# Attention's products in 64-row, 32-column tiles of TensorE, and six banks shared by scores and maxima

## The chip, the core and the metric

The kernel runs on one core of one Trainium2 chip. The metric is the device time of one execution in microseconds (us). The core has five engines with a queue each: TensorE (PE, whose weight loads are shown as PEld), VectorE (DVE), ScalarE (ACT), GpSimd (POOL) and SyncE (SP, which issues nearly all transfers). They meet through semaphores. Matmul results land in PSUM, 8 banks of 128 partitions x 512 fp32 numbers; ACT and DVE read them there.

## The reference, cut to what matters

A transformer block over 2048 rows of 512 numbers: attention with 32 heads of 16 numbers, then a gated MLP with a spatial mixing matrix. The change is in the attention.

```
H = 32; Dh = D // H
qkv = (LN(x) @ wqkv).reshape(B, S, 3, H, Dh)
scores = einsum("bhqd,bhkd->bhqk", q, k) * Dh ** -0.5
p = softmax(scores, axis=-1)
o = einsum("bhqk,bhkd->bhqd", p, v)
h = x + o.reshape(B, S, D) @ wo
```

## The kernel before

Each number of q and k is carried as fp16 parts, so a head has 48 rows of contraction instead of 16. Two more rows subtract the largest score of a query, scaled, so that Exp can't overflow. One operand tile holds two heads at partitions 0 to 49 (t = 0) and two at partitions 64 to 113 (t = 1).

The attention is a loop over 512 units (8 groups of four heads, 4 blocks of 512 queries, 16 blocks of 128 keys), two units at a time: a **pair**. One block of 512 queries is 8 pairs. In each pair the program issues, in an order written out by hand in the list `PAIR`:

- 8 score products (tokens `s0` to `s7`, line 805): 50 rows x 128 keys by 512 queries, each into a bank of its own of the pool `ps_s` (3 banks in turn). ACT turns each into Exp (line 814), which is stored in SBUF as `pt`.
- 8 products for the row maxima of a later block of queries (tokens `M0` to `M7`, line 223): into four banks `m0` to `m3` in turn (`bank`, `ps_m`, and one bank of `ps_m3`). DVE reduces 6 of them (line 228), ACT takes the absolute value of one (line 233), and DVE joins that with the eighth in a two-input reduction (line 237) that ends with a read of its accumulator.
- the weighted values (`weigh`, line 830, tokens `H`, `H`, `P`): for two blocks of keys, four fp32 matmuls of 128 keys x 32 columns, one for each head of the group, which add up in one bank `pv` over all 16 blocks of keys. Token `H` does 256 of the 512 queries, `P` all.

After the last block of keys DVE copies `pv` to SBUF (`take`, line 840, token `out`), and SP stores it. POOL meanwhile prepares weights for the MLP (`work`), off this chain.

Every PSUM result has a tile of its own with one bank. Semaphores come from the tile framework: it orders any two instructions that use one tile when one of them writes it, and lets instructions on different tiles run freely. All engines run their queues in the order of the program.

The products for maxima run ahead: 11 of 256 sets are made before the loop (`LEAD`), so 245 pairs have all 16 products, one pair has 8 scores alone, and the last 10 pairs run in another form (`scores2`, line 823): two scores into one tile of two banks, and one Exp over 1024 numbers, between matmuls for the next layer (`make_h`, line 747).

Of the kernel before, what the change touches and what calls it, by code (L numbers as in the profile page):

```python
# [39 lines left out]
PAIR = "s0 M0 join s2 M4 M1 s1 H s3 invert M2 s5 M3 H out M5 s4 M7 turn s6 s7 M6 P".split()  # L40
# [19 lines left out]
def block_kernel(ctx: ExitStack, tc: tile.TileContext, x, wqkv, wo, w_in, w_sp4, b_sp, w_out, out):  # L60
# [144 lines left out]
    def max_pair(m):  # L205

        g, i = divmod(m, 8)
        hg, qb = divmod(g, NQ)
        q, k, w = qst[g], kst[hg % 2], uvs[hg % 2]
        if i == 0:
            mx[g] = sm.tile([P, 16, 4], F32, name="mx")
            nc.gpsimd.memset(mx[g][:, :8, 3:], LOW)
        c, p = slice(i % 4 * P, i % 4 * P + P), i // 4
        at = lambda t, e: mx[g][:, t * 8 + i, e:e + 1]

        def scores(t, keys, b):  # L220
            r = slice(RG * t, RG * t + KS)
            acc = bank(b)
            nc.tensor.matmul(acc, q[r, p, c], keys[r, p], start=True, stop=True)  # L223
            return acc

        def one(t, e, b):
            acc = scores(t, k[:, :, 512 * e:512 * e + 512], b)
            nc.vector.reduce_max(at(t, e if t else e - 1), acc, axis=AX.X)  # L228

        def minus(b):  # L230
            acc = scores(0, w[:, :, 512:], b)
            ab[0] = sm.tile([P, 512], F32, name="ab")
            nc.scalar.activation(ab[0], acc, AF.Abs)  # L233

        def plus(b):
            acc = scores(0, w[:, :, :512], b)
            nc.vector.tensor_tensor_reduce(ab[0], acc, ab[0], 0.5, LOW, ALU.add, ALU.max, at(0, 0))  # L237
# [12 lines left out]
        ab = {}  # L250
        four = [lambda b, e=e: one(1, e, b) for e in range(4)]
        two = [lambda b, e=e: one(0, e, b) for e in (2, 3)]
        return [four[0], two[0], two[1], minus, four[1], four[2], plus, four[3], finish]

# [533 lines left out]
    with ExitStack() as at:  # L788
# [4 lines left out]
        pp = at.enter_context(tc.tile_pool(name="pp", bufs=6))  # L793
        ps_v = at.enter_context(tc.tile_pool(name="ps_v", bufs=1, space=PSUM))
        inner = at.enter_context(ExitStack())
        ps_m3 = inner.enter_context(tc.tile_pool(name="ps_m3", bufs=1, space=PSUM))
        ps_s = inner.enter_context(tc.tile_pool(name="ps_s", bufs=3, space=PSUM))
        more.clear()
        more[3] = lambda: ps_m3.tile([P, 512], F32, name="m3")
        pv = {}  # L800

        def product(s, hg, qb, kb, p, t):

            r = slice(RG * t, RG * t + KM)
            nc.tensor.matmul(s, kst[hg % 2][r, p, kb * P:(kb + 1) * P],  # L805
                             qst[hg * NQ + qb][r, p, :], start=True, stop=True)

        def score(hg, qb, kb, p, t):
# [3 lines left out]
            s = ps_s.tile([P, 512], F32, name="s")  # L812
# [3 lines left out]
        def scores2(hg, qb, kb, p):  # L816

            pts[p, kb] = pp.tile([P, 2, 512], F32, name="pt")
            turn[0] += 1
            s = later[turn[0] % 3 != 1].tile([P, 2, 512], F32, name="s2")  # L820
# [4 lines left out]
        def weigh(hg, qb, kb, a=0, b=512):  # L825
            if kb == 0:
                pv[0] = ps_v.tile([P, 512], F32, name="pv")
            for j in range(4):
                c = (4 * kb + j) * VW
                nc.tensor.matmul(pv[0][32 * j:32 * j + 32, a:b], vst[hg % 2][:, c:c + 32],  # L830
                                 pts[j % 2, kb][:, j // 2, a:b], start=kb == 0, stop=kb == NB - 1,
                                 skip_group_check=True)
            if b == 512:
                for p in range(2):
                    del pts[p, kb]

        def take(hg, qb, pool=sm):

            o = pool.tile([P, 512], F32, name="og", bufs=2)
            nc.vector.tensor_copy(o, pv[0])  # L840
# [204 lines left out]
        for n in range(0, len(units), 2):  # L1045
# [15 lines left out]
            steps = max_pair(m) if m < 8 * HG * NQ else []  # L1061
            m += 1
            if not steps and not later:
                maxima.close()
                later.append(attn.enter_context(
                    tc.tile_pool(name="ps_l", bufs=1, space=PSUM, side="right")))
                steps_h.append(make_h(h_rows[0], later[0].tile([P, 512], F32, name="h")))
            elif not steps and len(later) == 1:
                inner.close()
                later.append(at.enter_context(tc.tile_pool(name="ps_t", bufs=2, space=PSUM)))  # L1070
# [13 lines left out]
            if len(later) == 2:  # L1084
                if turned:
                    max_rows()
                more_h = n in (492, 494, 508, 510)
                scores2(hg, qb, kb, 0)
                scores2(hg, qb, kb, 1)
                some_h(1 + more_h)  # L1090
                weigh(*prev)
                if ends:
                    take(*prev[:2])
                scores2(hg, qb, kb1, 0)
                scores2(hg, qb, kb1, 1)
                some_h(1)
                weigh(hg, qb, kb)
            first = True
            for tok in PAIR if len(later) < 2 else ():
                i = int(tok[-1]) if tok[-1].isdigit() else 0  # L1100
                if tok[0] == "s":
                    score(hg, qb, (kb, kb1)[i // 4], i % 4 // 2, i % 2)
                elif tok[0] == "M" and steps:
                    steps[i](count[0] % 4)
                    count[0] += 1
                    if i == 6:
                        joins.append(steps[8])
                elif tok == "join":
                    join()
                elif tok == "H" and prev is None:  # L1110
                    if first:
                        pv[0] = ps_v.tile([P, 512], F32, name="pv")
                        for j in range(4):
                            nc.tensor.matmul(pv[0][32 * j:32 * j + 32, :], vst[0][:, :32],
                                             vst[0][:, :512], start=True, stop=True)
                    first = False
                elif tok == "H":
                    a = 0 if first else 256
                    weigh(*prev, a, a + 256)
                    first = False  # L1120
                elif tok == "P":
                    weigh(hg, qb, kb)
                elif tok == "out" and ends:
                    take(*prev[:2])
                elif tok == "invert" and kb == 6 and n > NB:
                    invert()
                elif tok == "turn" and turned:
                    max_rows()
            prev = (hg, qb, kb1)
# [8 lines left out]
            if n == 500:  # L1138
                steps_h.append(make_h(h_rows[1], later[0].tile([P, 512], F32, name="h")))
            if n == 502:  # L1140
                new_hn(h_rows[0])
        weigh(*prev)
# [461 lines left out]
```

## Time and profile before

| | |
|---|---|
| time, median of 3 runs | 1713.79 us (1713.14 to 1713.97) |
| span of the profiled execution | 1712.3 us, about 1.5 us less than the median time |
| before the attention's loop | 0 to 160 us |
| the 245 pairs with scores and maxima | 160 to 1249 us |
| 11 last pairs of the attention | 1249 to 1294 us |
| the MLP | from 1294 us on |

The page gives each engine's busy share, the span in 40 slices, the chain of work that ended last, and groups of instructions by line. A group's row has: line, engine, operation, output <- inputs, shapes and count, then busy us and mean ns of one, then the idle time of the engine just before them and who ended it. A row of the timeline has: start, length, engine, line, operation, and how many instructions were merged into it; merged ones overlap, so the length of a row divided by its count is less than one instruction takes. "PEclk" is the granted clock of TensorE as a share of full speed.

### The profile page before, as it was taken

How to read it: one execution, taken by the hardware profiler on the slowest of the kernel's cores; microseconds unless marked ns; L12 is line 12 of the kernel's file. 1: busy time of each engine (PE TensorE's matmuls, PEld its weight loads, DVE VectorE, ACT ScalarE, POOL GpSimd, SP SyncE). 2: the span in 40 equal slices, each digit the busy share in tenths (PEclk: the TensorE clock that was granted, in tenths of full speed). 3: DMA queues.
4: the chain of work that ended last, by engine and by line, in shares of the span. 5: the costliest groups of instructions: out<-in, count | busy, mean ns of one | idle time of the engine just before them, and what ended most of it. 6: DMA issues, size and time to landing. Idle time of an engine off the chain costs nothing.

```text
span 1712.3 us, 36689 instructions
## 1 busy us (share of the span) xinstructions
PE 1699.5 (99%) x13508; PEld 644.7 (38%) x13508; DVE 1452.5 (85%) x3051; ACT 1317.5 (77%) x2584; POOL 813.6 (48%) x1062
## 2 busy tenths in 40 slices
PE   9999999999999999999999999999999999999999
PEld 4533222222222222222222222222225666656665
DVE  7688999999999999999999999999936787543444
ACT  4334999999999999999999999999995545211111
POOL 1231867776673267687767776400002766300100
PEclk9999999999999999999999999999999999999999
DMA  5534332342221244344434444300114454664551
GB/s 185 167 94 144 103 89 68 101 94 82 81 68 25 56 118 117 104 144 125 130 113 124 132 140 130 80 13 19 37 39 124 140 173 140 233 234 156 198 217 44
DMA packets 189309, 196.03 MB, mean 114 GB/s; under 512 B 67496, under 2 KB 140008, under 8 KB 189128
## 3 DMA queue, kind: packets, MB, share of 16 engines
q1 hardware_dynamic: 186824, 188.04, 36.8%
q10 hardware_dynamic: 2304, 5.64, 0.8%
q8 instruction: 106, 1.74, 0.4%
q14 instruction: 75, 0.61, 0.1%
HBM read 122.10 MB, written 65.93 MB: 110 GB/s over the span
## 4 chain that ended last, share of the span: by engine, by line
PE 78%; DVE 12%; DMA 3%; POOL 2%; ACT 2%; SPq 2%; issue 1%; ACTq 0%; POOLq 0%; DVEq 0%
PE pv L830 26%; PE s L805 17%; PE m L223 9%; DVE mx L228 7%; PE acc L107 4%; PE g L108 4%; PE g L109 4%; PE g L107 4%; PE acc L109 4%; PE acc L108 4%; DMA rc<-r_scr 1%; DVE ab L237 1%; DVE og L840 1%; SPq L723 1%; DVE rs_t L124 1%
## 5 line engine op out<-in xcount | busy, mean ns | idle before, releaser
L814 ACT ACTIVATE pt<-s 128x512 f32<-128x512 f32 x1968 | 1006.2, 637 | 5.5 <-PE m L223 4.3
L228 DVE TENSOR_REDUCE mx<-m 128x1 f32<-128x512 f32 x1510 | 947.5, 682 | 11.7 <-PE m L223 2.9
L805 PE MATMUL s<-qst,kst 50*128 50x512 f16 x2048 | 604.2, 379 | 0.2
L830 PE MATMUL pv<-pt,vst 128*32 128x256 f32 (+1 forms) x6056 | 598.1, 466 | 4.1 <-DVE og L840 1.3
L223 PE MATMUL m<-kst,qst 48*128 48x512 f16 x1510 | 452.4, 381 | 0.0
L805 PEld LDWEIGHTS <-kst 50*128 50x128 f16 x2048 | 132.0, 94 | 352.1 <-issue 323.7
L830 PEld LDWEIGHTS pv<-pt,vst 128*32 128x32 f32 x6056 | 119.5, 108 | 290.7 <-issue 277.3
L223 PEld LDWEIGHTS <-qst 48*128 48x128 f16 x2048 | 159.2, 93 | 173.6 <-issue 124.2
L223 PE MATMUL m<-uvs,qst 48*128 48x512 f16 x504 | 190.5, 380 | 0.6 <-DVE mx L228 0.6
L245 POOL TENSOR_SCALAR nm<-nm 128x16 f32<-128x16 f32 x32 | 6.6, 206 | 358.8 <-DVE nm L242 358.8
L237 DVE CUSTOM_DVE_ANT_0 ab<-m,ab 128x512 f32<-128x512 f32 x252 | 170.5, 677 | 2.7 <-ACT ab L233 2.7
L233 ACT ACTIVATE ab<-m 128x512 f32<-128x512 f32 x252 | 157.3, 624 | 15.5 <-PE m L223 14.8
L1368 ACT ACTIVATE pr<-pr,up 128x304 f32<-128x304 f32 (+1 forms) x32 | 17.0, 574 | 109.2 <-DVE up L1322 109.2
L991 POOL TENSOR_TENSOR op<-raw,op 128x512 f16<-128x512 f32 x80 | 92.9, 1161 | 6.0
L914 POOL TENSOR_TENSOR raw<-raw 128x512 f32<-128x512 f32 (+1 forms) x84 | 83.3, 991 | 6.7
L919 POOL TENSOR_TENSOR acc_sp<-acc_sp,raw 128x512 f32<-128x512 f32 x63 | 80.4, 1277 | 4.5
L109 PE MATMUL acc<-wi,hT 128*128 128x344 f16 x256 | 79.1, 309 | 0.3 <-DVE hT L104 0.3
L107 PE MATMUL acc<-wi,hT 128*128 128x344 f16 x256 | 79.1, 309 | 0.0
L108 PE MATMUL acc<-wi,hT 128*128 128x344 f16 x256 | 79.1, 309 | 0.0
L1510 POOL TENSOR_TENSOR pr<-pr,z 128x344 f32<-128x344 f32 x8 | 7.3, 914 | 145.9 <-DMA whole<-squares 108.3
L911 POOL TENSOR_SCALAR raw<-raw 128x512 f32<-128x512 f32 (+1 forms) x88 | 52.3, 594 | 19.7 <-DMA raw<-in_wqkv 12.4
L1509 DVE TENSOR_TENSOR pr<-g,v 128x344 f32<-128x344 f32 x8 | 4.1, 517 | 66.6 <-PE g L109 63.5
(247 smaller groups left out, 2292.9 us busy)
## 6 DMA issues: line engine op xcount, KB each, us to landing
raw<-in_w_sp SPq DMA_DIRECT2D x128, 256.0 KB
s_scr<-op SPq DMA_DIRECT2D x64, 256.0 KB
op<-s_scr SPq DMA_DIRECT2D x32, 512.0 KB
a_scr<-op SPq DMA_DIRECT2D x48, 256.0 KB
op<-a_scr SPq DMA_DIRECT2D x24, 512.0 KB
o_scr<-og SPq DMA_DIRECT2D x64, 128.0 KB
qst<-q_scr SPq DMA_DIRECT2D x192, 32.0 KB
kst<-k_scr SPq DMA_DIRECT2D x48, 128.0 KB
```

The costliest lines, as they stand in the source:

```text
L107: nc.tensor.matmul(ps, lh, rh, start=first, stop=False, **kw)
L108: nc.tensor.matmul(ps, lh, rl, start=False, stop=False, **kw)
L109: nc.tensor.matmul(ps, ll, rh, start=False, stop=last, **kw)
L223: nc.tensor.matmul(acc, q[r, p, c], keys[r, p], start=True, stop=True)
L228: nc.vector.reduce_max(at(t, e if t else e - 1), acc, axis=AX.X)
L233: nc.scalar.activation(ab[0], acc, AF.Abs)
L237: nc.vector.tensor_tensor_reduce(ab[0], acc, ab[0], 0.5, LOW, ALU.add, ALU.max, at(0, 0))
L805: nc.tensor.matmul(s, kst[hg % 2][r, p, kb * P:(kb + 1) * P], qst[hg * NQ + qb][r, p, :], start=True, stop=True)
L814: nc.scalar.activation(pts[p, kb][:, t, :], s, AF.Exp, scale=scales_[hg // 2])
L830: nc.tensor.matmul(pv[0][32 * j:32 * j + 32, a:b], vst[hg % 2][:, c:c + 32], pts[j % 2, kb][:, j // 2, a:b], start=kb == 0, stop=kb == NB - 1,
L914: pool.tensor_mul(got[0] if n else acc, got[0], got[0])
L991: chores.append((lambda: pool.tensor_sub(t[0][:, 1], of(), t[0][:, 0]), TT))
```

## The change

Four things change in the attention's loop; the last one follows from the others.

1. **Quarters.** A score product or maxima product is issued as four matmuls of 32 columns of the stationary operand (`by_quarters`), each onto 32 partitions of the result. With the 64-row halves that the operands already use, every product then has the form 64 rows x 32 columns.
2. **Two sums.** `weigh` splits the 128 keys of a block into keys 0 to 63 and 64 to 127 and adds each half up in a bank of its own (`pv0`, `pv1`), in halves of 256 queries. At the end of a block ACT copies `pv1` to SBUF (`take_half`), and DVE adds it to `pv0` (`take`) in place of its copy.
3. **Six banks in turn.** One tile `slots` of six banks takes the place of the three `s` banks and the four `m` banks. Each product takes the bank that was given out longest ago. In the last pairs two neighbouring banks are taken at once, and one bank is held for `make_h`.
4. **The order.** `PAIR` is written anew, with a second list `FIRST_PAIR` for the first pair of a block of queries. In the lists `N` is a product of the t = 1 heads that DVE reduces, `n` one of t = 0, `A` the product for ACT's absolute value and `C` the one for the two-input reduction; `Q0`, `Q1` and `R0`, `R1` are the two sums for the block of keys before and for this one.

```diff
-PAIR = "s0 M0 join s2 M4 M1 s1 H s3 invert M2 s5 M3 H out M5 s4 M7 turn s6 s7 M6 P".split()
+PAIR = "s1 s0 N n s3 Q0 Q1 s2 N A Q1 s4 N Q0 s5 n R1 C s7 R0 R1 s6 N turn R0 rows".split()
+FIRST_PAIR = "s1 n N s0 s2 Q1 Q0 s3 n Q1 Q0 half N s4 out A s5 N s6 R1 C R1 R0 s7 N turn R0".split()
+SLOTS = 6
...
+    class Slots:
+        def __init__(self, pool, n):
+            self.acc = pool.tile([P, n, 512], F32, name="slots")
+            self.used, self.now = [0] * n, 0
...
+        def one(self):
+            i = min(range(len(self.used)), key=self.used.__getitem__)
+            self.mark(i)
+            return self.acc[:, i, :]
...
+    def by_quarters(acc, left, right):
+        for c in range(4):
+            c = slice(32 * c, 32 * c + 32)
+            nc.tensor.matmul(acc[c], left[:, c], right, start=True, stop=True)
...
         def scores(t, keys, b):
             r = slice(RG * t, RG * t + KS)
-            acc = bank(b)
-            nc.tensor.matmul(acc, q[r, p, c], keys[r, p], start=True, stop=True)
+            if slots:
+                acc = slots.one()
+                by_quarters(acc, q[r, p, c], keys[r, p])
...
-        ps_s = inner.enter_context(tc.tile_pool(name="ps_s", bufs=3, space=PSUM))
+        slots = Slots(at.enter_context(tc.tile_pool(name="ps_s", bufs=1, space=PSUM)), SLOTS)
...
-            s = ps_s.tile([P, 512], F32, name="s")
+            s = slots.one()
             product(s, hg, qb, kb, p, t)
             nc.scalar.activation(pts[p, kb][:, t, :], s, AF.Exp, scale=scales_[hg // 2])
...
-            s = later[turn[0] % 3 != 1].tile([P, 2, 512], F32, name="s2")
+            s = slots.two()
...
-        def weigh(hg, qb, kb, a=0, b=512):
+        def weigh(hg, qb, kb, t, cols=256):
...
+            r, c = slice(RG * t, RG * t + RG), slice(a, a + cols)
             for j in range(4):
...
+                nc.tensor.matmul(pv[t][32 * j:32 * j + 32, c], vst[hg % 2][r, v:v + 32],
+                                 pts[j % 2, kb][r, j // 2, c], start=kb == 0 and not a,
+                                 stop=kb == NB - 1 and a + cols == 512,
+                                 tile_position=(RG * t, 32 * j), skip_group_check=True)
...
+        def take_half(pool=sm):
+            halves.append(pool.tile([P, 512], F32, name="half", bufs=1))
+            nc.scalar.activation(halves[0], pv[1], AF.Copy)
...
-            nc.vector.tensor_copy(o, pv[0])
+            nc.vector.tensor_add(o, pv[0], halves.pop())
...
-                elif tok == "H" and prev is None:
-                    if first:
-                        pv[0] = ps_v.tile([P, 512], F32, name="pv")
-                        for j in range(4):
-                            nc.tensor.matmul(pv[0][32 * j:32 * j + 32, :], vst[0][:, :32],
-                                             vst[0][:, :512], start=True, stop=True)
```

What the change does to the instructions is shown by the built programs, engine by engine. Each row is one instruction with its line (in the changed file `by_quarters` is line 237, the Exp line 851, the reductions lines 266 and 275, the absolute value line 271, `weigh` line 870), output <- inputs and size, and behind it the engines whose semaphores it waits for.

First PE, in a pair from the middle of the attention. Before, the products of the first group of a pair stand as follows; `s` and `m_...` are tiles of one bank, `kst` and `qst` the operands:

```order
L805 LDWEIGHTS kst_158
L805 MATMUL s<-qst,kst_158 128x512 [waits Activation_49]
L223 LDWEIGHTS qst
L223 MATMUL m_11665<-kst_158,qst 128x512 [waits DVE_49]
L223 LDWEIGHTS qst
L223 MATMUL m_11668<-kst_158,qst 128x512 [waits DVE_49]
L805 LDWEIGHTS kst_158
L805 MATMUL s<-qst,kst_158 128x512 [waits Activation_49]
L830 MATMUL pv<-pt,vst_156 32x256 x4
```

A score waits for ACT, whose Exp frees the `s` banks, and a maxima product for DVE, which frees the `m` banks. With the change, the end of a first pair of a block (tokens `s6`, `R1`, `C`, `R1`, `R0`, `s7`, `N`) has these rows, of which the second to fourth quarter of each product are left out:

```order
L237 MATMUL slots<-qst,kst_158 32x512 [waits DVE_49]
...
L870 MATMUL pv_19306<-pt,vst_156 32x256 x3
L237 LDWEIGHTS qst
L237 MATMUL slots<-uvs_159,qst 32x512 [waits Activation_49]
...
L870 MATMUL pv_19306<-pt,vst_156 32x256 x4
L870 MATMUL pv_19320<-pt,vst_156 32x256 [waits PE_49]
...
L237 MATMUL slots<-qst,kst_158 32x512 [waits DVE_49]
...
L237 MATMUL slots<-kst_158,qst 32x512 [waits Activation_49]
```

The engine that a product waits for is now the reader of the product issued just before it: `s6` waits for DVE (which reduces the `N` before it), `C` (the row with `uvs`) for ACT (Exp of `s6`), `s7` for DVE (which reduces `C`), and `N` for ACT (Exp of `s7`). The readers of the banks' contents of six products earlier would be, for `C`, DVE, and for `s7`, ACT. The counts that these semaphores must reach say the same: in the pairs with all 16 products every product waits for the instruction that reads the product before it.

Then ACT at the same stage. Before, one pair and the next:

```order
L814 ACTIVATE pt<-s 128x512 [waits PE_49] x8
L233 ACTIVATE ab<-m_3962 128x512 [waits PE_49]
L814 ACTIVATE pt<-s 128x512 [waits PE_49] x8
L233 ACTIVATE ab<-m_4031 128x512 [waits PE_49]
L814 ACTIVATE pt<-s 128x512 [waits PE_49] x8
```

With the change, one pair:

```order
L851 ACTIVATE pt<-slots 128x512 [waits PE_49]
L271 ACTIVATE ab<-slots 128x512 [waits DVE_49,PE_49]
L851 ACTIVATE pt<-slots 128x512 [waits PE_49,Activation_49]
L851 ACTIVATE pt<-slots 128x512 [waits DVE_49,PE_49]
L851 ACTIVATE pt<-slots 128x512 [waits DVE_49,PE_49,Activation_49]
L851 ACTIVATE pt<-slots 128x512 [waits PE_49]
```

An Exp waited for its product alone; now those behind a product that DVE reads wait for DVE as well, though they read another bank. On DVE the reductions turn from the first form into the second in the same way:

```order
L228 TENSOR_REDUCE mx<-m_12819 128x1 [waits PE_49]
L228 TENSOR_REDUCE mx<-m_12832 128x1 [waits PE_49]
L228 TENSOR_REDUCE mx<-m_12847 128x1 [waits PE_49]
L228 TENSOR_REDUCE mx<-m_12853 128x1 [waits PE_49]
L237 ISA ab,mx<-m_12863,ab 128x512 [waits PE_49,Activation_49]
```

```order
L266 TENSOR_REDUCE mx<-slots 128x1 [waits PE_49,Activation_49] x2
L266 TENSOR_REDUCE mx<-slots 128x1 [waits PE_49]
L266 TENSOR_REDUCE mx<-slots 128x1 [waits PE_49,Activation_49] x3
L275 ISA ab,mx<-slots,ab 128x512 [waits DVE_49,PE_49]
L275 ISA mx 128x1
```

All banks of scores and maxima are now parts of one tile, and the waits stand between neighbours in the program, whichever banks they use.

More of the change, by code (lines that the diff above doesn't have):

```diff
@@ L250, in max_pair @@
         ab = {}
[L251 to L252 removed]
+        four = [lambda b=None, e=e: one(1, e, b) for e in range(4)]
+        two = [lambda b=None, e=e: one(0, e, b) for e in (2, 3)]
+        if slots:
+            return {"N": four, "n": two, "A": [minus], "C": [plus], "end": finish}
         return [four[0], two[0], two[1], minus, four[1], four[2], plus, four[3], finish]
@@ new lines, in block_kernel @@
+                weigh(hg, qb, kb, 1, 512)
+                weigh(hg, qb, kb, 0, 512)
+            for tok in (FIRST_PAIR if ends else PAIR) if len(later) < 2 else ():
+                t = int(tok[-1]) if tok[-1].isdigit() else 0
+                if tok[0] == "s" and len(tok) == 2:
+                    score(hg, qb, (kb, kb1)[t // 4], t % 4 // 2, t % 2)
+                elif tok in ("A", "C", "N", "n"):
+                    if steps:
+                        steps[tok].pop(0)()
+                elif tok[0] == "Q" and prev:
+                    weigh(*prev, t)
+                elif tok[0] == "R":
+                    weigh(hg, qb, kb, t)
+                elif tok == "half":
+                    take_half()
+                elif tok == "out":
+                    take(*prev[:2])
+                elif tok == "rows":
+                    join()
+                    if kb == 6 and n > NB:
+                        invert()
```

103 lines of the change are left out of this document (46 added, 57 removed).

## The prediction

> **What bounds the kernel now.** I read the engines' shares and the chain first, then the costliest groups.
>
> ```profile
> span 1712.3 us, 36689 instructions
> PE 1699.5 (99%) x13508; PEld 644.7 (38%) x13508; DVE 1452.5 (85%) x3051; ACT 1317.5 (77%) x2584; POOL 813.6 (48%) x1062
> PE 78%; DVE 12%; DMA 3%; POOL 2%; ACT 2%; SPq 2%; issue 1%; ACTq 0%; POOLq 0%; DVEq 0%
> L814 ACT ACTIVATE pt<-s 128x512 f32<-128x512 f32 x1968 | 1006.2, 637 | 5.5 <-PE m L223 4.3
> L228 DVE TENSOR_REDUCE mx<-m 128x1 f32<-128x512 f32 x1510 | 947.5, 682 | 11.7 <-PE m L223 2.9
> L823 ACT ACTIVATE pt<-s 128x1024 f32<-128x1024 f32 x40 | 37.6, 1021 | 0.9 <-ACT pt L814 0.3 <-PE s L805 0.2
> ```
>
> The chain runs through PE for 78% of the span. But the share of one stage counts here, so I asked for the busy time in a stretch of the attention.
>
> ```profile
> core 0: us, PE busy (x) PEld busy (x) DVE busy (x) ACT busy (x) POOL busy (x), PEclk, DMA share, GB/s
> 600.00:700.00 100.00, 99.66 (x904) 28.19 (x905) 99.25 (x194) 99.95 (x205) 72.66 (x104) 1.00 0.40 112
> ```
>
> PE, DVE and ACT are all above 99%: three engines in balance. Nothing that helps PE alone can be worth much, and anything that stops the three from working at the same time costs nearly all of what it stops. The timeline shows how they run side by side; first the stage's two ends and the fp32 product that opens a pair:
>
> ```profile
> 160.23 0.39 PE L805 MATMUL s<-qst,kst 50*128 50x512 f16 x1
> 604.31 1.06 PE L830 MATMUL pv<-pt,vst 128*32 128x512 f32 x8
> 608.72 1.06 PE L830 MATMUL pv<-pt,vst 128*32 128x512 f32 x8
> 1249.46 0.39 PE L805 MATMUL s<-qst,kst 50*128 50x512 f16 x1
> ```
>
> A pair takes 608.72 - 604.31 = 4.41 us; over the 245 pairs with all 16 products, (1249.46 - 160.23) / 245 = **4.45 us** a pair, 1089 us in all. In 4.41 us 16 products are made and read, one each 0.28 us. A single one, from its start to the end of its reader, takes four times as long, as the next rows show. The kernel lives by having several banks in flight.
>
> **What the change takes away from that.** The built program of the change says that each product waits for the reader of the product before it, whatever its bank. All six banks are one tile, and the waits are made for the tile. So I price a chain of 16 links a pair instead of 4.45 us. One link is: product starts, its reader starts, the reader ends, the next product starts. Its three parts stand in these rows.
>
> ```profile
> 160.66 1.57 ACT L814 ACTIVATE pt<-s 128x512 f32<-128x512 f32 x3 [2.26 <-PE m L223]
> 161.63 0.60 ACT L814 ACTIVATE pt<-s 128x512 f32<-128x512 f32 x1
> 161.67 0.68 DVE L228 TENSOR_REDUCE mx<-m 128x1 f32<-128x512 f32 x1
> 605.15 0.68 DVE L237 CUSTOM_DVE_ANT_0 ab<-m,ab 128x512 f32<-128x512 f32 x1
> 605.75 0.08 DVE L237 DVE_READ_ACCUMULATOR2_ANT mx<- 128x1 f32 x1
> 604.76 1.13 ACT L814 ACTIVATE pt<-s 128x512 f32<-128x512 f32 x2
> 605.95 0.37 PE L805 MATMUL s<-qst,kst 50*128 50x512 f16 x1
> ```
>
> - Product to reader: at the start of the loop ACT had been idle for 2.26 us; the product began at 160.23 and its Exp at 160.66, so 0.43 us.
> - Reader: an Exp without another close behind took 0.60, the group's mean is 0.637; I take 0.62. A reduction takes 0.68. The two-input one ends with its accumulator's read, 605.75 + 0.08 - 605.15 = 0.68.
> - Reader to the next product: two Exps ended at 604.76 + 1.13 = 605.89, and the score that needed the bank began at 605.95, so 0.05 to 0.06; I take 0.05.
>
> Nine of a pair's readers are on ACT (8 Exps and an absolute value): 9 x (0.43 + 0.62 + 0.05) = 9.9 us. Seven are on DVE: 7 x (0.43 + 0.68 + 0.05) = 8.1 us. Sum **18.0 us**.
>
> Two small costs are added to links. The quarters start one after the other, and the reader waits for the fourth. Reductions now wait for two engines, one of them through an instruction of its own on the queue.
>
> ```profile
> 161.87 0.19 PEld L1114 LDWEIGHTS pv<-vst 128*32 128x32 f32 x8 [1.31 <-PE s L805]
> L840 DVEq EVENT_SEMAPHORE  x20: 21/36/50, 305.1 to 1252.8; - x20
> L830 PEld LDWEIGHTS pv<-pt,vst 128*32 128x32 f32 x6056 | 119.5, 108 | 290.7 <-issue 277.3
> ```
>
> Eight loads of 32 columns lasted 0.19 us in all, one of them 0.108: they start some 0.08 / 7 = 0.01 us apart, so the fourth quarter is about 0.03 us late. The semaphore instruction takes 21 to 50 ns. The bounds are 0 and 0.1 us a link; I take 0.045, which is 0.7 us a pair, so **18.7 us** (bounds 18.0 and 19.6). Below 18.0 it could get only if readers were at their shortest and the parts overlapped; 17.0 is my floor.
>
> The rest of the loop hides in this chain. The longest weighted sums between two links are `R0` and `R1` behind `s7`:
>
> ```profile
> 601.84 0.64 PE L830 MATMUL pv<-pt,vst 128*32 128x256 f32 x8
> 602.41 0.39 PE L805 MATMUL s<-qst,kst 50*128 50x512 f16 x1
> 602.64 0.38 PE L805 MATMUL s<-qst,kst 50*128 50x512 f16 x1
> ```
>
> A half of 256 queries holds PE 602.41 - 601.84 = 0.57 us, changes of form included, and a product 0.23. Even one after the other 0.23 + 0.57 = 0.80 is less than a link of 1.10, and the two sums lie in different rows. The sums' split, the new order and the larger number of matmuls therefore cost nothing while the chain lasts. ACT's copy of `pv1` (0.60, a form like the Exp's) stands between two links that DVE reads, beside DVE's 1.16; without that cover it would cost 0.6 x 31 = 19 us. DVE's addition takes the place of a copy beside an Exp. POOL and SP are given the same work in four times the time. What the change removes on PE (the changes of form, up to 0.57 - 2 x 0.23 = 0.11 us at each weighted half) is off the path now, so it gains nothing.
>
> The end of the attention: the pair with scores alone is 8 x 1.10 = 8.8 us in place of 4.4, and the last ten pairs have four links of two scores and a wide Exp (1.02 by its group), 4 x (0.45 + 1.02 + 0.05) = 6.1 us. The two matmuls of `make_h` write the held bank of the same tile and come between links, 2 x 0.23 and the change of form, 0.6. So 6.7 against 37.6 / 10 = 3.8 us: 10 x 2.9 + 4.4 = 33 us. A placeholder product at the start goes, 1 us.
>
> The sum: 245 x (18.7 - 4.45) = 3491, and 32, is 3523 us over the execution's span of 1712.3, which is 1.5 us less than the median of the runs shown: **about 5240 us**.
>
> **The clock.** In a chain PE is idle most of the time. By the rows above it streams 16 products of 0.23 us and some sums, 5 to 6 of 18.7 us, with pauses under 1 us. What that does to its clock no stage of this trace shows. Two ends of it bear on the question.
>
> ```profile
> 1707.58:1710.99 3.41, 1.14 (x9) 1.00 0.43 154
> 1711.00:1712.20 1.20, 0.00 (x0) 0.50 0.00 0
> L526 PE MATMUL acc<-idle 128*128 128x512 bf16 x8 | 3.4, 610 | 1.2 <-DVE idle L520 1.2
> L526 PE MATMUL acc<-idle 128*128 128x512 bf16 x18 | 4.1, 384 | 0.0
> ```
>
> At the end, after 3.4 us in which PE was busy for 1.14 (33%), the granted clock fell to 0.50. At the start, the first eight matmuls (1.0 to 4.3 us) took 610 ns in the mean and those from 4.5 us on 384: a slow clock adds 0.23 to 0.25 us to a product. Whether 30% in short pieces counts as idle is open. I forecast with full clock, since the pause at the end was one piece of over 1 us, and ours are shorter.
>
> [...]
>
> **The rivals.**
>
> *The clock falls, for all or part of the loop.* For it: PE's share would be about that of the stretch before the fall. Against: no single long pause. All products slow: 16 x 0.24 = 3.8 us a pair, 245 x 3.8 = 940 us more, 6180 us; with swings in between, 5700.
>
> *The waits bind by bank after all, and the change does what it says: faster.* Then a product waits for the reader of six products ago, six links' time is spread over six products, and PE, without changes of form, has room. What is left is ACT: two Exps together took 1.13 us, so 1.13 - 0.637 = 0.49 each, 0.48 by the tighter of such rows.
>
> ```profile
> 604.28 1.12 ACT L814 ACTIVATE pt<-s 128x512 f32<-128x512 f32 x2
> ```
>
> 1.12 - 0.637 = 0.48; 9 x 0.48 and an eighth of the copy's 0.48 are 4.38 us against 4.45, so 245 x 0.07 = 17 us less at best, and some lost to waits: 1700 us. It decides at one point, whether the wait before a product is for its own bank's reader. For it speaks only the change's intent; against it the semaphores of the built program, which point to the neighbour in all 245 pairs. [...]
>
> *The chain is looser.* If a wait or two in a pair falls to another engine's earlier work, a pair is 17.0 us: 245 x 12.55 + 32 = 3107, 4820 us.
>
> **How the numbers follow.** Forecast, full clock, 5240 us (its own range 4820 to 5460 by 17.0 and 19.6 us a pair): 0.52. Slow or swinging clock, 5700 to 6180: 0.40. Faster by free banks, 1700: 0.06. Something in which the change costs less than a few hundred us: 0.02. Leaving out the free banks and the tail above, the range is 4900 to 6350 us, the upper end a slow clock with half the extra cost of links. By 0.2%, about what a measurement of this kernel tells from no change: faster 0.06, same 0.01, slower 0.93.
>
> **What would show it.** In the profile of the changed kernel the 245 pairs would take 18 to 19 us each; ACT and DVE would be busy for about 9 x 0.62 and 7 x 0.68 us of that, a third and a quarter; the chain would go from product to Exp or reduction to product, with nearly every product's idle time ended by ACT or DVE, and reductions and Exps never side by side. Products of 0.38 us mean full clock, of 0.63 the slow one. The forecast is wrong if Exps and reductions still overlap, or if a link is not 1.1 to 1.2 us.

## The result, and the profile after

| | before | after |
|---|---|---|
| time, median | 1713.88 us (1713.14 to 1714.39, 4 runs) | 6107.84 us (6105.34 to 6110.01, 4 runs) |
| ratio | | 3.564, 95% interval 3.559 to 3.569 |
| span of the profiled execution | 1712.3 us | 6103.6 us |
| mean granted clock of TensorE | 1.00 | 0.55 |

Kernels given below without an interval ran once. `six_whole`, near the end, is the only one with executions over 1.5% slower than its fastest, and its ratio leaves these out.

The kernel is 3.6 times slower. The forecast (5240 us) had the direction and the mechanism; of its two clocks it took the wrong one. The rival with the slow clock (6180) is what happened.

First the page of the changed kernel: span, the engines' shares, the granted clock in 40 slices, the chain of waits by engine, and the two groups of readers.

```profile
span 6103.6 us, 83375 instructions
PE 3882.3 (64%) x35516; PEld 1032.2 (17%) x35516; DVE 1592.3 (26%) x3051; ACT 1572.7 (26%) x2616; POOL 810.2 (13%) x1062
PEclk9555555555555555555555555555555555555999
PE 57%; DVE 20%; ACT 18%; issue 5%; DVEq 0%; POOL 0%; ACTq 0%; POOLq 0%
L851 ACT ACTIVATE pt<-slots 128x512 f32<-128x512 f32 x1968 | 1175.4, 597 | 3574.9 <-PE slots L237 3574.9
L266 DVE TENSOR_REDUCE mx<-slots 128x1 f32<-128x512 f32 x1470 | 1017.1, 692 | 3991.5 <-PE slots L237 3991.5
```

The two readers' groups are little busier than before (1175 us for 1006, and 1017 for 947); it is their idle time that has grown, from 5.5 and 11.7 us to 3575 and 3992, and the product ends it. DVE and ACT now stand in the chain with 20% and 18%, where they had 12% and 2%, and PE with 57% in place of 78%. And the clock is at half speed in all slices of the attention.

The absolute value on ACT comes once a pair, so its first and last start give the pair's length (the row has count, shortest/median/longest ns, first and last start). Before:

```profile
L233 ACT ACTIVATE ab<-m x245: 603/620/642, 164.3 to 1248.0; 128x512 f32<-128x512 f32 x123
```

After:

```profile
L271 ACT ACTIVATE ab<-slots x245: 597/597/598, 169.7 to 5578.2; 128x512 f32<-128x512 f32 x123
```

245 starts are 244 pairs: (1248.0 - 164.3) / 244 = 4.44 us before, (5578.2 - 169.7) / 244 = **22.17 us** after. That is 244 x 17.725 = 4325 of the 4391 us by which the span grew; 61 lie behind the last of these starts (1712.3 - 1248.0 = 464 us before, 6103.6 - 5578.2 = 525 after), 5 ahead of the first. Of the 61, 10 still belong to the last pair: its successor, the pair with scores alone, begins at 1249.46 before and at 5589.99 after, so the stretch from there on has grown by 51 (462.8 to 513.6).

Now the links of the chain, in the timeline of the changed kernel: the first three products of the loop, and two links in its middle.

```profile
160.13 0.40 PE L237 MATMUL slots<-qst,kst 50*32 50x512 f16 x4
160.58 0.60 ACT L851 ACTIVATE pt<-slots 128x512 f32<-128x512 f32 x1 [2.28 <-PE slots L237]
161.23 0.40 PE L237 MATMUL slots<-qst,kst 50*32 50x512 f16 x4 [0.70 <-ACT pt L851]
162.32 0.40 PE L237 MATMUL slots<-kst,qst 48*32 48x512 f16 x4 [0.69 <-ACT pt L851]
162.83 0.69 DVE L266 TENSOR_REDUCE mx<-slots 128x1 f32<-128x512 f32 x1 [1.18 <-PE slots L237]
163.57 0.61 PE L237 MATMUL slots<-kst,qst 48*32 48x512 f16 x4 [0.86 <-DVE mx L266]
...
3010.75 0.61 PE L237 MATMUL slots<-qst,kst 50*32 50x512 f16 x4 [0.69 <-ACT ab L271]
3011.41 0.60 ACT L851 ACTIVATE pt<-slots 128x512 f32<-128x512 f32 x1 [0.71 <-PE slots L237]
3012.06 0.62 PE L237 MATMUL slots<-kst,qst 48*32 48x512 f16 x4 [0.69 <-ACT pt L851]
3012.79 0.69 DVE L266 TENSOR_REDUCE mx<-slots 128x1 f32<-128x512 f32 x1 [4.17 <-PE slots L237]
3013.53 0.61 PE L237 MATMUL slots<-qst,kst 50*32 50x512 f16 x4 [0.86 <-DVE mx L266]
```

No two readers overlap. The three first products (0.40 us for four quarters) show the chain at full clock: 161.23 - 160.13 = 1.10 us with an Exp, 163.57 - 162.32 = 1.25 with a reduction. The fourth product takes 0.61: the granted clock has fallen to 0.50, and it stays there to the loop's end (0.50 over all of 163.81 to 5590 us). From there the links are 3012.06 - 3010.75 = 1.31 and 3013.53 - 3012.06 = 1.47. A pair of nine and seven is 9 x 1.10 + 7 x 1.25 = **18.65 us** at full clock and 9 x 1.31 + 7 x 1.47 = 22.08 at half clock; 22.17 was measured.

### The profile page after: what moved, and what is told of

Its sections match the earlier page's. It is cut to its first block, busy times and chain, and to the rows that moved or that the text cites. A ratio compares the mean times of both kernels' runs of the same rounds, so it can differ in the third digit from the quotient of the medians.

```text
span 6103.6 us, 83375 instructions
## 1 busy us (share of the span) xinstructions
PE 3882.3 (64%) x35516; PEld 1032.2 (17%) x35516; DVE 1592.3 (26%) x3051; ACT 1572.7 (26%) x2616; POOL 810.2 (13%) x1062
## 3 DMA queue, kind: packets, MB, share of 16 engines
q8 instruction: 278, 4.55, 0.3%
## 4 chain that ended last, share of the span: by engine, by line
PE 57%; DVE 20%; ACT 18%; issue 5%; DVEq 0%; POOL 0%; ACTq 0%; POOLq 0%
PE slots L237 40%; DVE mx L266 17%; ACT pt L851 15%; PE pv L870 7%; DVE ab L275 3%; ACT ab L271 2%; PE acc L109 2%; PE acc L111 1%; PE acc L110 1%; PE g L110 1%; PE g L111 1%; PE g L109 1%; PE acc L787 1%; ACT pt L859 0%; DVEq L266 0%
## 5 line engine op out<-in xcount | busy, mean ns | idle before, releaser
L851 ACT ACTIVATE pt<-slots 128x512 f32<-128x512 f32 x1968 | 1175.4, 597 | 3574.9 <-PE slots L237 3574.9
L266 DVE TENSOR_REDUCE mx<-slots 128x1 f32<-128x512 f32 x1470 | 1017.1, 692 | 3991.5 <-PE slots L237 3991.5
L870 PE MATMUL pv<-pt,vst 64*32 64x256 f32 (+1 forms) x16048 | 1787.3, 635 | 0.0
L237 PE MATMUL slots<-qst,kst 50*32 50x512 f16 x8192 | 1229.0, 594 | 861.0 <-DVE mx L266 419.7
L237 PE MATMUL slots<-kst,qst 48*32 48x512 f16 x5880 | 901.4, 598 | 1057.0 <-ACT pt L851 845.4
L237 PEld LDWEIGHTS <-kst 50*32 50x32 f16 x8192 | 404.1, 100 | 2271.4 <-issue 2270.9
L237 PEld LDWEIGHTS <-qst 48*32 48x32 f16 x7840 | 340.3, 97 | 2445.8 <-issue 2445.7
L237 PE MATMUL slots<-uvs,qst 48*32 48x512 f16 x1960 | 300.2, 598 | 295.6 <-DVE mx L266 267.3
L870 PEld LDWEIGHTS pv<-pt,vst 64*32 64x32 f32 x16048 | 407.0, 140 | 91.1 <-issue 90.3
L275 DVE CUSTOM_DVE_ANT_0 ab<-slots,ab 128x512 f32<-128x512 f32 x245 | 169.5, 692 | 217.1 <-PE slots L237 217.1
```

The lines of the kernel that those rows point to most:

```text
L237: nc.tensor.matmul(acc[c], left[:, c], right, start=True, stop=True)
L851: nc.scalar.activation(pts[p, kb][:, t, :], s, AF.Exp, scale=scales_[hg // 2])
L870: nc.tensor.matmul(pv[t][32 * j:32 * j + 32, c], vst[hg % 2][r, v:v + 32], pts[j % 2, kb][r, j // 2, c], start=kb == 0 and not a, stop=kb ...
```

## The experiments

### Is it the tile?

My theory: the six banks are one tile, the waits are made for the tile, and that alone puts all products in a row. Rival: the quarters, the two sums or the new order cost the time. Three kernels tell them apart. The first is the changed kernel with each bank a tile; its last ten pairs take their banks one by one.

```diff
-            self.acc = pool.tile([P, n, 512], F32, name="slots")
+            self.acc = [pool.tile([P, n // TILES, 512], F32, name=f"slots{i}") for i in range(TILES)]
...
-            return self.acc[:, i, :]
+            return self.acc[i % TILES][:, i // TILES, :]
```

With TILES = 6 (`six_tiles`):

> The changed kernel, with each of the six banks a tile of its own; the last ten pairs take their banks one by one, with an Exp of 512 numbers each. Theory (the waits of the one tile cost the time): a product now waits for the reader of six products before, the chain of 16 links is gone, and a pair is bound by ACT, 4.4 us; 1700 us, between 1690 and 1740, the clock at 1.00 in the loop. Rival (the quarters, the two sums or the new order cost it by themselves): over 2000 us still.

1764.23 us, ratio 1.031 (1.029 to 1.033). 4344 us of the loss go with that edit. The rest of the expectation was too good: 1764, not 1690 to 1740 (below). The same edit with TILES = 2:

> As six_tiles, but with two tiles of three banks, which products take in turn, so that a product waits for the reader of the product two before. Theory: half of the chain, (9 x 1.10 + 7 x 1.26) / 2 = 9.35 us a pair at full clock, 1712 + 245 x (9.35 - 4.45) = 2910 us; at the slow clock 22.2 / 2 = 11.1 us and 3340 us. Rival (the cost has nothing to do with the tiles): about 6100 us as before it.

3484.51 us, mean clock 0.59, and a pair of (2959.1 - 165.0) / 244 = 11.45 us by the same row of its trace: half of the chain at half clock (11.1), 3% longer. The dose follows the distance of the wait. Then the other way round, the kernel before with its seven banks made one tile (in the last ten pairs, which have no maxima, three score banks stand by themselves again):

```diff
-        ps_m3 = inner.enter_context(tc.tile_pool(name="ps_m3", bufs=1, space=PSUM))
-        ps_s = inner.enter_context(tc.tile_pool(name="ps_s", bufs=3, space=PSUM))
+        ps_s = inner.enter_context(tc.tile_pool(name="ps_s", bufs=1, space=PSUM))
...
-        more[3] = lambda: ps_m3.tile([P, 512], F32, name="m3")
+        all_ = ps_s.tile([P, 7, 512], F32, name="all")
+        for i in range(4):
+            more[i] = lambda i=i: all_[:, 3 + i, :]
...
-            s = ps_s.tile([P, 512], F32, name="s")
+            s = all_[:, turns[0] % 3, :]
```

> The kernel before, with nothing changed but its three score banks and four maxima banks made one tile. No quarters, no second sum, the old order. Theory (the one tile does it): the chain of 16 links again, 18.0 to 18.7 us a pair at full clock (5030 to 5200 us), 21.5 to 22.2 at the slow clock (5890 to 6060 us). Rival (quarters, sums or order do it): about 1714 us, and by a part of each less than 3000.

6154.87 us, a pair of (5678.6 - 173.4) / 244 = 22.56 us, a little over my 21.5 to 22.2 for the slow clock, and the time over my 5890 to 6060. Its rows say the same as those of the changed kernel:

```profile
L228 DVE TENSOR_REDUCE mx<-all 128x1 f32<-128x512 f32 x1470 | 1016.5, 691 | 3434.3 <-PE all L223 3434.3
L233 ACT ACTIVATE ab<-all x245: 597/597/597, 173.4 to 5678.6; 128x512 f32<-128x512 f32 x123
```

So the merged tile is enough for the whole loss, without any quarter, second sum or new order, and taking it apart is enough to undo all but 50 us. That settles the cause.

### Is the rest the clock, and why does it fall?

The changed kernel again, one tile as it is, with work added that nobody needs: matmuls of zeros behind each product (four banks in turn make room; the waits stay).

```diff
+        for _ in range(IDLE):
+            nc.tensor.matmul(spare[0], zeros[0][:, :P], zeros[0], start=True, stop=True)
```

With two of them:

> The changed kernel, one tile as it is, with two more matmuls of 128 x 128 by 512 bf16 zeros behind each product, into a bank that nobody reads (four banks in turn instead of six, which changes no wait). They add work to PE where it waits. Theory (the slow clock is what took the time from 5240 to 6108 us, and it comes from PE's low share): PE is busy for over 60% of each link, the clock stays at 1.00, a pair is 18.65 us, and the time falls to about 5220 us although PE does more. Rival (the clock falls for another reason, the pauses for the readers themselves): the clock stays at 0.50, and three matmuls of 0.43 us in a link make it 6100 to 6600 us.

5374.82 us: with two more full matmuls for each product the kernel is 733 us faster. The windows of PE (start:end, length, PE busy and count, granted clock, share of DMA, GB/s) show why. First the changed kernel, then this one:

```profile
160.40:163.81 3.41, 1.16 (x16) 0.92 0.60 200
163.81:167.22 3.41, 1.60 (x12) 0.50 0.72 238
2500.00:4000.00 1500.00, 896.79 (x8666) 0.50 0.09 25
```

```profile
160.40:163.81 3.41, 1.79 (x12) 1.00 0.49 166
163.81:167.22 3.41, 2.68 (x19) 1.00 0.85 258
2500.00:4000.00 1500.00, 1288.21 (x12355) 1.00 0.11 31
L276 ACT ACTIVATE ab<-slots x245: 597/597/600, 169.6 to 4823.1; 128x512 f32<-128x512 f32 x123
```

At full clock a pair is (4823.1 - 169.6) / 244 = 19.07 us, the chain's 18.65 and some 0.4, which I put down to products that stand behind fillers. With the end of the attention, where the fillers stand too, that is 155 us over the expected 5220. That a matmul which does nothing useful saves time shows that the slow clock was the rest of the loss, and that more work on PE kept the clock from falling. The fillers raise PE's share and shorten its pauses at once, so which of the two counts isn't told apart. One filler instead of two:

> chain_filled with one matmul of zeros behind each product instead of two. Theory (a share between that of the chain alone and that of the chain with two fillers is enough; the last pairs of the changed kernel kept 1.00 in windows with PE busy 1.83 to 1.89 of 3.41 us): clock 1.00, 18.7 to 19.0 us a pair, 5250 to 5320 us. Rival (it is not enough; in two_tiles the clock fell in a window with 1.96 of 3.41): clock 0.50, 22.2 to 22.6 us a pair, 6110 to 6250 us.

6596.38 us, a miss for my theory and over the rival's numbers too. The clock fell here as well, a little later, and a pair is (6038.9 - 171.5) / 244 = 24.05 us. At half clock the filler pushes the sums behind it into the next product: in this trace a filler starts at 3004.05 us, the sums at 3004.59, and the Exp of 3004.22 ends at 3004.82, but the next product starts at 3005.45, 0.63 us after that Exp, where in the changed kernel that took 0.05 (3011.41 + 0.60 to 3012.06).

```profile
160.40:163.81 3.41, 1.52 (x12) 1.00 0.62 210
163.81:167.22 3.41, 2.35 (x14) 0.63 0.61 196
2500.00:4000.00 1500.00, 1268.72 (x8834) 0.50 0.08 23
L276 ACT ACTIVATE ab<-slots x245: 597/597/598, 171.5 to 6038.9; 128x512 f32<-128x512 f32 x123
```

A window's mean clock tells when the fall came: the traces of before and after have no values but 1.00 and 0.50, and I take the others to be alike. In the changed kernel 0.92 means 0.55 us at half clock, so it fell at about 163.3 us, and in the 3.41 us before that (159.88 to 163.29) PE was busy for 1.44. Here 0.63 means 2.5 us at half clock, a fall at about 164.7, so most of this window's 2.35 us belong to the slow clock; in the window before it PE was busy for 1.52 of 3.41.

No share in PE's busy column divides the two clocks. In `two_tiles` the clock fell at the end of a window with 1.96 of 3.41 us (the first row below), while two late windows of the changed kernel kept full clock with less:

```profile
160.40:163.81 3.41, 1.96 (x28) 0.96 0.64 214
5645.57:5648.98 3.41, 3.34 (x34) 0.57 0.55 92
5648.98:5652.40 3.42, 1.83 (x40) 1.00 0.40 114
5652.40:5655.81 3.41, 1.89 (x34) 1.00 0.00 0
```

And in the trace of `six_whole`, a kernel with separate tiles that comes up again below, the clock was at 0.50 here (0.86 in the mean over that execution), with PE's records covering all of the time and ACT and DVE idle for half of it (this row has PE, PEld, DVE, ACT and POOL ahead of the clock):

```profile
600.00:700.00 100.00, 100.00 (x762) 19.32 (x759) 46.64 (x81) 48.85 (x88) 25.79 (x30) 0.50 0.15 35
```

So PE's records can show it busy for all of 100 us while the clock stays at 0.50. One reason why the column says so little: a product's record (0.38 us) is longer than the 0.23 us after which the next one started (602.41 and 602.64 in the trace of before), and longer still at half clock (0.61 for four quarters, 0.40 at full clock), so the column overstates a chain of single products. What makes the clock fall stays open.

### What keeps the separate tiles from being faster?

`six_tiles` still lost 3.1%. Its waits of PE between 200 and 1240 us (who waited for whom: total us, times, longest; in its file L232 is `by_quarters`, L846 the Exp, L261 a reduction, L862 `weigh`):

```profile
PE slots L232 <- DMA qst<-m_scr: 14.7, 19, 1.9
PE slots L232 <- issue: 6.6, 5, 2.4
PE slots L232 <- ACT pt L846: 5.6, 9, 0.6
PE pv L862 <- issue: 5.1, 9, 1.2
```

The first row is a block's maxima on their way into the operand. The new order finishes them at the end of a pair (`rows`), the old one early in it (`join`). So I moved the token:

```diff
-PAIR = "s1 s0 N n s3 Q0 Q1 s2 N A Q1 s4 N Q0 s5 n R1 C s7 R0 R1 s6 N turn R0 rows".split()
+PAIR = "rows s1 s0 N n s3 Q0 Q1 s2 N A Q1 s4 N Q0 s5 n R1 C s7 R0 R1 s6 N turn R0".split()
```

> six_tiles with the token rows at the head of the list PAIR instead of its end, so that the maxima of a block are finished, turned and sent to the operand one pair (4.4 us) earlier. In six_tiles the first product of a block waited for that transfer (PE idle for qst<-m_scr, 19 times, 14.7 us in all, up to 1.9 us), and ACT and DVE ran dry behind it; its blocks took 36.3 to 40 us against 35.49. Theory (the late transfer is what is left of the loss): the stall goes, blocks take 35.0 to 35.5 us, 1700 to 1718 us. Rival (quarters, two sums or the first pair's own order cost it): blocks stay above 36, over 1735 us.

1748.43 us, ratio 1.020 (1.019 to 1.022): 16 us of the hoped-for 46 to 64, and in the rival's range (over 1735). The waits for `qst<-m_scr` were gone, but new ones stood there: the division had moved with the token, and DVE waited for its sums.

```profile
DVE rcp L812 <- DMA sums<-o_scr: 6.1, 5, 1.9
```

> six_early with only the end of the maxima at the head of the list; the division (rcp, line 812), which in six_early had moved up with it and made DVE wait for sums<-o_scr (6.1 us in five waits), stands at the end again. Theory (that wait was a part of the 35 us that six_early lost): the waits of rcp go, 1748 less 6 to 10, so 1737 to 1744 us. Rival (others fill its place): within 0.2% of 1748.

1740.16 us, ratio 1.015 (1.014 to 1.017), as expected. What PE waits for now:

```profile
PE pv L862 <- issue: 8.5, 9, 2.1
PE slots L232 <- issue: 5.0, 5, 1.7
PE slots L232 <- DVE mx L261: 1.0, 3, 0.6
```

"issue" means that nothing in the profile releases it. The longest, in the timeline:

```profile
834.93 0.62 PE L862 MATMUL pv<-pt,vst 64*32 64x256 f32 x3
...
837.67 0.41 PE L862 MATMUL pv<-pt,vst 64*32 64x256 f32 x3 [2.13 <-issue]
```

PE stops in the midst of four like matmuls, of which none waits for a semaphore. Number all of PE's instructions in this trace from 0: matmuls, weight loads and the few that wait for a semaphore. All 17 of PE's pauses of over 0.25 us between 200 and 1245 us, 15.9 us in sum, stand at numbers such as 31425, 35009, 39617 and 41665, each 193 more than a multiple of 256. PE has 35516 matmuls here where it had 13508, and the page has a DMA queue for the instructions themselves. Before and `six_split`:

```profile
q8 instruction: 106, 1.74, 0.4%
```

```profile
q8 instruction: 278, 4.55, 1.1%
```

That is 4.55 / 1.74 = 2.6 times the bytes, for 35516 / 13508 = 2.6 times the matmuls. That PE's instructions come in blocks, and that a pause is a block that comes late, is my estimate from the places of the pauses and these bytes; no view shows a block arrive. In a pair the trace has 256 of PE's instructions, where it had 80; my 192, 160 and 56 below count an fp32 matmul once, and it stands in the trace as two. The test puts the other transfers away:

```diff
-            if m % 8 and n < 480:
-                work(4.1 if m % 8 < 7 else 2.0)
```

> six_split with all of POOL's preparation of the MLP's weights, and its DMAs, put off from the pairs to the end of the loop (n = 480), where it piles up, so that only the loop's pairs are compared, not the whole time. In six_early PE stood still for up to 2.2 us without waiting for a semaphore, at matmuls and loads whose number from the start is 193 or 194 more than a multiple of 256, most of them between 600 and 1050 us, where the weights are loaded. Theory (PE's instructions arrive in blocks, and late where the weights' transfers use the same DMA engines): PE's pauses of over 0.3 us without a semaphore go, and nearly all blocks of 8 pairs take 35.8 us. Rival (the blocks come late by themselves, PE asking for 192 instructions a pair instead of some 56): the pauses stay, as long and as many.

Between 200 and 1245 us all of PE's pauses of over 0.25 us went. Measured from one absolute value on ACT to that eight pairs later, 27 of the loop's first 29 blocks took 35.5 to 35.8 us and two 36.0 and 36.2, where `six_split` had blocks of up to 38.5. (The whole, 2383.77 us, has the put-off work at its end.) So the pauses come with the preparation of the weights, in a kernel that executes 256 PE instructions in a pair of 4.41 us; that they are instructions coming late fits, but stays my estimate. The edit puts off POOL's work together with its transfers; that the transfers are what delays the instructions is likely, since these are transferred too (the 4.55 MB), but not shown by itself. Nor was it tried whether the transfers' queues or the memory behind them is the narrow place.

What remains is 35.77 against 35.49 us a block, 0.28 x 31 = 9 us. I put it down to ACT's copy of the second sum, a term that the forecast priced at 19 if uncovered; no run takes the copy out alone. The other 18 or so of the 26 us are close to the 15.9 us of those pauses. Two attempts to win back a part failed. A fresh tile for each product, so that a reader needn't wait for the other engine's earlier read of the same tile:

```diff
-            i = min(range(len(self.used)), key=self.used.__getitem__)
-            self.mark(i)
-            return self.acc[i % TILES][:, i // TILES, :]
+            return self.pool.tile([P, 512], F32, name="slots")
```

> six_split with a new tile of one bank for every product (a pool of six), as the kernel before has it for its own banks, instead of six tiles used over and over. A reader then waits for its product alone, not for the other engine's earlier read of the same tile too; these second waits cost an instruction of 17 ns on ACT, where Exps stood 0.487 to 0.494 us apart in place of 0.477. Theory (the second waits keep a pair at 4.41): a pair falls towards 9 x 0.477 = 4.30 us, 245 x 0.02 to 0.11 = 5 to 25 us less than 1740, so 1715 to 1735 us. Rival (DVE or the order holds the pair at 4.41): 1740 within 0.2%.

1742.25 us, ratio 1.017 (1.015 to 1.018), the rival's value. The edit did less than I expected: between 200 and 1200 us the extra semaphore instructions of DVE's one-input reductions went (604 to none), but on ACT 1104 of 1289 stayed. Those that went cost nothing that shows. That the rest cost little is likely: in the trace of before ACT has none of them, and its Exps stand 0.478 us apart in the median, some 0.494, much as here. But no run takes them all away. And with fewer instructions, each sum in one piece of 512 queries (the lists then have one token for each sum in place of two):

```diff
-        def weigh(hg, qb, kb, t, cols=256):
+        def weigh(hg, qb, kb, t, cols=512):
```

> six_fresh with each sum in one piece of 512 queries instead of two of 256, 160 instead of 192 PE instructions a pair. Theory (the late blocks of PE's instructions are some 18 us of what is left): a sixth fewer blocks, and with that 3 us less at least than six_fresh. Rival (a piece of 0.86 us holds products and readers up): 5 to 40 us more than six_fresh.

1811.90 us, ratio 1.057 (1.056 to 1.059). PE had no pause for issue left, with 192 instructions in a pair by the trace, but the pair took 4.82 us: ACT waited 48.9 us for products behind the long pieces. That is the rival, and 70 us more than `six_fresh` where it had 5 to 40.

### What the parts are worth

Two more kernels take one part out of `six_early`. Without the quarters:

```diff
-        for c in range(4):
-            c = slice(32 * c, 32 * c + 32)
-            nc.tensor.matmul(acc[c], left[:, c], right, start=True, stop=True)
+        nc.tensor.matmul(acc, left, right, start=True, stop=True)
```

> six_early with each product as one matmul of 128 columns again; the two sums stay. It prices the quarters. Theory (the quarters let a product in one half of the rows run beside a sum in the other, and save changes of form): without them each of the eight pieces of the sums, about 0.43 us, stands by itself on PE beside 16 products of 0.216 us, up to 6.9 us a pair and with changes of form 7.5, so 2300 to 2500 us. Rival (the quarters do little): within 2% of six_early, about 1710 to 1740 us.

Ratio 1.226 (1.224 to 1.228), so 1.226 x 1713.38 = 2101 us; with 387 us more over 245 pairs that is 4.44 + 1.58 = 6.0 us a pair, less than my 6.9 to 7.5, and a time under my 2300 to 2500. Without the second sum:

```diff
-                nc.tensor.matmul(pv[t][32 * j:32 * j + 32, c], vst[hg % 2][r, v:v + 32],
-                                 pts[j % 2, kb][r, j // 2, c], start=kb == 0 and not a,
+                nc.tensor.matmul(pv[0][32 * j:32 * j + 32, c], vst[hg % 2][:, v:v + 32],
+                                 pts[j % 2, kb][:, j // 2, c], start=kb == 0 and not a,
```

> six_early with one sum over 128 keys in one bank, as before the change; the quarters of the products stay. It prices the two sums. Theory (with quarters alone PE still changes form at each sum, 8 times a pair at 0.09 us, but products in the two halves of the rows can overlap): PE stays the bound or near it, 1705 to 1740 us. Rival (the two sums are needed, PE is held by 128-row sums between quarters): over 1760 us.

1920.75 us, ratio 1.121 (1.120 to 1.123): the rival. Not all of it is PE's form: with one bank for the sum and the new list, the first sum of a block also waits for DVE's copy of the last one (22.8 us in 22 waits between 200 and 1240 us). Its timeline shows what a change of form costs, and that two products in the two halves of the rows run side by side:

```profile
643.73 0.64 PE L864 MATMUL pv<-pt,vst 128*32 128x256 f32 x8
644.30 0.40 PE L232 MATMUL slots<-uvs,qst 48*32 48x512 f16 x4
644.32 0.40 PE L232 MATMUL slots<-qst,kst 50*32 50x512 f16 x4
644.64 0.64 PE L864 MATMUL pv<-pt,vst 128*32 128x256 f32 x8
645.21 0.40 PE L232 MATMUL slots<-qst,kst 50*32 50x512 f16 x4
```

From two products to the next sum it is 644.64 - 644.32 = 0.32 us where a product holds PE for 0.23, so 0.09 for the change of form. The two products start 0.02 us apart and share that time. In the new order, taking out the quarters thus costs about 353 us and taking out the second sum 172, against `six_early`; one alone is worse than none in the old order (1714). With both, PE has room in a pair (busy for 97.29 of 100 us in `six_split`, 1100 to 1200 us, 99.66 before); but ACT (100.00) and DVE (99.60) were bounds beside it, and a pair of `six_split` takes 4.41 us in the median, as before the change. No version beat the kernel before.

## Why the prediction was right, and where not

- **A chain of 16 links** in place of banks side by side: right, shown by `six_tiles`, `two_tiles` and `merged_before`.
- **The price of a link at full clock**, 1.10 and 1.16 us and 0.045 for small costs, 18.7 us a pair: right in sum, 18.65. The small costs lie otherwise: none on links with an Exp, 0.09 on links with a reduction. `chain_filled` ran the chain at full clock in 19.07.
- **The rest of the loop hides in the chain:** right. Links and measurement differ by 0.09 us a pair (22.08 and 22.17).
- **Full clock:** wrong, the step of the forecast that failed. It read: "I forecast with full clock, since the pause at the end was one piece of over 1 us, and ours are shorter." The pauses here are 0.69 to 0.86 us, and the clock fell 3.2 us into the loop, after 3.41 us in which PE was busy for 1.44. The row quoted from the end of the trace before, 1.14 of 3.41 and then 0.50, was the better evidence: a like share. The price of the slow clock was in the rival's sum with 0.24 us a product; it is 1.31 - 1.10 = 0.21 and 1.47 - 1.25 = 0.22. Its 6180 came out only 72 us high because two errors have opposite signs: pairs of 18.7 + 3.84 = 22.54 us where 22.16 were measured, (5589.99 - 160.13) / 245, are 92 us too much, and the end of the attention was 18 too little.
- **A swinging clock, 5700 us:** no run of the chain shows that term in the pairs with scores and maxima. In the changed kernel the clock stayed at 0.50 in them after the fall, from 163.3 to 5590 us; it changed to and fro only in the last ten pairs (windows at 0.93, 0.50, 0.57 and 1.00 between 5608 and 5652 us).
- **The end of the attention:** 33 us forecast, 51 measured, a term too small; part of it ran at half clock (0.74 in the mean from 5600 to 5700 us).
- **Free banks, 1700 us, slightly faster:** not what the program asked for, as argued. Where the program does ask for it (`six_tiles`), it is 1764, because the maxima came late (`six_early`), PE paused without a semaphore (`six_late_work`), and, as argued above, ACT had a copy more.

## What to carry to other kernels

Before gathering buffers into one tile, ask what the framework takes as the unit of a wait: a tile of six banks was one buffer, and its index only looked like six. A chain through PE can cost twice, as here, once for its links (18.65 us a pair in place of 4.45) and again when the granted clock falls (3.4 more at 0.50); price both, and take a row with a like share of busy PE as evidence, however short. When matmuls are cut into quarters, count the instructions too (256 a pair here in place of 80).

## What the runs showed of the hardware that I had not expected

- Instructions are themselves a transfer (4.55 MB in `six_split`, 1.74 before), and PE paused where no semaphore held it: up to 2.1 us in `six_split`, each time at an instruction whose number is 193 more than a multiple of 256, gone when the preparation of the weights, with its transfers, was put off, and gone at 192 instructions in 4.82 us (`six_fewer`).
- Useless matmuls made the kernel 733 us faster (5374.82 against 6107.84), and one filler in place of two made it slower than none (6596.38).
- Once down, the clock did not rise for the chain: 0.50 through 1500 us of windows with PE's records busy 60% (896.79 of 1500), 85% with one filler (1268.72), and, with separate tiles, through 100 us at 100% (`six_whole`, 600 to 700 us).
- Matmuls of 64 rows x 32 columns in different row halves run side by side (0.02 us between starts in `six_onesum`); a change of form from them to 128-row matmuls costs 0.09 us there (0.32 less 0.23).
